# Banded attention with global keys and a two-matmul MoE layer: the second matmul of granules 4 to 11 as seven block products per granule pair

## The chip, the cores and the metric

The kernel runs on one core of one Trainium2 chip. The time is device microseconds of one execution; before the change it is 216.85 us, the median of three runs (216.78 to 217.0). The engines are called as the profile calls them: PE (TensorE, matrix multiply, with its weight loads as PEld), DVE (VectorE), ACT (ScalarE), POOL (GpSimd) and SP (SyncE, here only a queue that issues DMAs).

## The reference

Attention over 4 batches, 8 heads, 768 positions and 64 dimensions per head. A query sees the 96 positions up to and including its own, and the first 8 positions (global keys) always. A bias of minus a head's slope times the distance is added. The result, laid out as 3072 tokens of 512 features, goes through a feed-forward layer with a squared relu:

```python
scores = scale * q @ k.T + bias          # kept where global or local
a = softmax(scores); x = a @ v           # -> [3072, 512]
h = x @ w_in                             # [3072, 2048]
r = maximum(h, 0)
g = s * (r * r) + b
out = g @ w_out                          # [3072, 512]
```

## The kernel before

**Granules and steps.** The 3072 tokens are cut into 12 granules of 256 tokens (two blocks of 128), three to a batch. For attention a granule has four units, one per pair of heads. Two units are one step, so granule j fills steps 2j and 2j+1, and there are 24 steps (0 to 23). The program's order is written out by hand (`tc.manual_schedule()`), engine by engine; each engine works through its own list strictly in order and waits on semaphores.

**Attention.** `stage_S` multiplies queries and keys into the PSUM tile `ps_s` (L395), ACT takes the exponential into `pt` (L404), DVE multiplies with `tmpl`, the exponential of bias and mask (L411). `stage_A` multiplies `pt` with the values into `ps_av` (L446); the values carry a column of ones, so the row sum comes along. `normalize` takes its reciprocal (L419) and scales into `xn` (L420). From granule 4 on, `xn` is transposed to `xT` by DMAs on SP (L550), and the raw keys and queries too (`qk_by_dma`, L311).

A query block needs its own key block, and the block before it. The first rows of that earlier block lie outside the window, so their place is taken by the 8 global keys. For the granules that are not the first of their batch, `make_koff` and `make_voff` build these shifted blocks on DVE: a copy of the earlier block (L330 keys, L349 values) and then a copy of the 8 global columns or rows over it (L333, L353).

**The two MoE matmuls.** `p1_mm` is the first: eight groups per granule, each of two 128-column chunks of `w_in` times four 128-row parts of x, 256 tokens wide, so 8 matmuls of 128x256 (L566) into one PSUM bank. ACT applies the relu into `gT` (L576), DVE squares it in place (L579). `p2_mm` is the second: per block of 128 tokens, 16 matmuls of 128x512 (L611), with a block of `gT` as the stationary operand and `w_out` moving. `p2_out` scales by s and adds the vector `bvec` (b times the column sums of `w_out`) on DVE (L622) and stores 256 KB through SP (L631). `bvec` comes from `wsum_add` (L589, 15 additions spread through the opening) and `emit_bvec`. Granules 0 and 1 finish their second matmul before s and b are there, so `p2_hold` keeps the raw product and `p2_late` (L644) finishes it.

**PSUM.** Of eight banks, four hold scores (two units), one holds `ps_av`, and three (`ps_h`, tag `psh`) are shared by the groups of the first matmul, the second matmul and the transposes. A bank is handed on in the order in which the banks before were released in the program.

**A step.** `step(s, c0, c1, c2)` writes: the scores of step s+1 with their exponentials and masks; the pieces c0; `stage_A` of the step's first unit; the held-back outputs (`flush`); c1; `stage_A` of the second unit; c2 and, at a granule's end, `finish_granule` (transposes of `xn`, then the loads of the granule four ahead on POOL's queue). In the steady state a step has one `p2` block in c0 and two groups of the first matmul each in c1 and c2. After step 23 the rest of the MoE work follows without attention: the last block of granule 9, half of granule 10's first matmul, and granules 10 and 11. The very last block is cut by columns in 384 and 128 (`moe_p2_cols`, L668, L676).

Of the kernel before, what the change touches and what calls it, by code (L numbers as in the profile page):

```python
# [17 lines left out]
def kernel(  # L18
# [41 lines left out]
    gpool = ctx.enter_context(tc.tile_pool(name="gpool", bufs=4))  # L60
# [59 lines left out]
    for i in range(GB):  # L120
        f = work.tile([P, H, D], F32, name="first_v", tag="first_v", bufs=2)
        nc.sync.dma_start(f[:], rows_of(v, 0, i))
        first_v.append(f)
# [20 lines left out]
    idle = const.tile([P, 4 * P], BF16, name="idle")  # L144
# [20 lines left out]
    rel = const.tile([P, 2 * P], F32, name="rel")  # L165
# [25 lines left out]
    )  # L191
    ident_bf = const.tile([P, P], BF16, name="ident_bf")
    make_identity(nc, ident_bf[:])
    nat_tile(0)
    load_granule(1)
    for i in range(4):
        load_w_in(i, 4)
# [9 lines left out]
    base_bf = const.tile([P, 3, P], BF16, name="base_bf")  # L207
    nc.vector.tensor_copy(base_bf[:, 0, :], rel[:, 0:P])
    nc.vector.tensor_copy(base_bf[:, 1:3, :], rel[:].rearrange("p (a c) -> p a c", a=2))
    nc.vector.tensor_scalar_max(base_bf[0:NG, 0, :], base_bf[0:NG, 0, :], -float(NL))  # L210
    nc.vector.memset(base_bf[0:NG, 2, :], -float(NL))
    slopes = [float(2.0 ** (-8.0 * (h + 1) / H)) for h in range(H)]
    diag = const.tile([P, H, P], BF16, name="diag")
# [7 lines left out]
    tmpl = const.tile([P, H, 5, P], BF16, name="tmpl")  # L221

    def template(hs):
        for h in hs:
            nc.scalar.activation(tmpl[:, h, 0:3, :], base_bf[:, 0:3, :], ACT.Exp, scale=slopes[h])

    def template_rest(hs):
        nc.vector.tensor_copy(tmpl[:, hs, 3, :], tmpl[:, hs, 2, :])
        nc.scalar.copy(tmpl[:, hs, 4, :], tmpl[:, hs, 1, :])
# [14 lines left out]
    koff = {}  # L244
    voff = {}
# [9 lines left out]
    def qk_tile(b):  # L255
        if b not in qk:
            qk[b] = qkp.tile([P, 2, NB, HP, P], BF16, name="qk", tag="qk")
        return qk[b]

    def qk_by_pe(j, h2s=range(HP // 2), evac=(nc.vector.tensor_copy, nc.vector.tensor_copy)):  # L260
        b, g = divmod(j, NGR)
        t = qk_tile(b)
        for h2 in h2s:
            for n in range(2):
                ps = ps_h.tile([P, GB, 2, P], BF16, name="ps_t", tag="psh")
                for i in range(GB):
                    for c in range(2):
                        hp = 2 * h2 + c
                        nc.tensor.transpose(  # L269
                            ps[:, i, c, :],  # L270
                            nat[j][:, n, i, 2 * hp : 2 * hp + 2, :],
                            ident_bf[:],
                        )
                dst = t[:, n, g * GB : (g + 1) * GB, 2 * h2 : 2 * h2 + 2, :]
                if j == 0:

                    evac[n](
                        dst.rearrange("p b c (m s) -> p c b m s", s=GB),
                        ps[:].rearrange("p s c (b m) -> p c b m s", b=GB),
                    )  # L280
                else:
                    evac[n](dst, ps[:])

    def qk_block(j, i, evac):
        b, g = divmod(j, NGR)
        t = qk_tile(b)
        for n in range(2):
# [5 lines left out]
            evac[n](t[:, n, g * GB + i, :, :], ps[:])  # L293

    def qk_wide(j, n, evac):
        b, g = divmod(j, NGR)
        t = qk_tile(b)
# [6 lines left out]
        evac(t[:, n, g * GB : (g + 1) * GB, :, :], ps[:])  # L304

    def qk_by_dma(j):
        b, g = divmod(j, NGR)
        t = qk_tile(b)
        for i in range(GB):
            for n in range(2):  # L310
                nc.sync.dma_start_transpose(  # L311
                    t[:, n, g * GB + i, :, :],
# [4 lines left out]
    def make_koff(j, blocks=range(GB), h2=None, copy=nc.vector.tensor_copy, splice=True):  # L317
        b, g = divmod(j, NGR)
        if g == 0:
            return  # L320
        r0 = g * GB - 1
        t = qk_tile(b)
        if j not in koff:
            koff[j] = work.tile([P, GB, HP, P], BF16, name="koff", tag="koff", bufs=2)
        ko = koff[j]
        hs = slice(0, HP) if h2 is None else slice(2 * h2, 2 * h2 + 2)
        nh = HP if h2 is None else 2
        i0, n = blocks[0], len(blocks)
        if copy:
            copy(ko[:, i0 : i0 + n, hs, :], t[:, 0, r0 + i0 : r0 + i0 + n, hs, :])  # L330
        if not splice:
            return
        nc.vector.tensor_copy(  # L333
            ko[:, i0 : i0 + n, hs, 0:NG],
            t[:, 0, 0, hs, 0:NG].unsqueeze(1).to_broadcast((P, n, nh, NG)),
        )

    def make_voff(j, blocks=range(GB), copy=nc.vector.tensor_copy, splice=True):
        b, g = divmod(j, NGR)
        if g == 0:  # L340
            return
        r0 = g * GB - 1
        vn = vbuf[b % 2]
        if j not in voff:
            voff[j] = work.tile([P, GB, H, VW], BF16, name="voff", tag="voff", bufs=2)
        vo = voff[j]
        i0, n = blocks[0], len(blocks)
        if copy:
            copy(vo[:, i0 : i0 + n, :, :], vn[:, r0 + i0 : r0 + i0 + n, :, :])  # L349
        if not splice:  # L350
            return
        for i in blocks:
            nc.vector.tensor_copy(vo[0:NG, i, :, :], vn[0:NG, 0, :, :])  # L353

    def stage_S(u):
        j, hp, b, g = unit(u)
        t = qk_tile(b)
# [8 lines left out]
        c0 = 0 if first else 1  # L368
# [11 lines left out]
        plan = [(i, t[:, 0, r0 + i, hp, :], t[:, 1, r0 + i, hp, :]) for i in range(GB)]  # L380
        if first:
            plan.append((2, t[:, 0, 0, hp, :], t[:, 1, 1, hp, :]))
        else:
# [3 lines left out]
                (1, koff[j][:, 0, hp, :], t[:, 1, r0, hp, :]),  # L387
                (2, koff[j][:, 1, hp, :], t[:, 1, r0 + 1, hp, :]),
# [36 lines left out]
    def stage_A(u, pool=None):  # L425
# [10 lines left out]
        dcol, ocol = ((0, 1), (None, 2)) if first else ((0, 3), (1, 2))  # L436
        for i in range(GB):
            for hi in range(2):
                h = 2 * hp + hi
                terms = [(dcol[i], vn[:, g * GB + i, h, 0 : D + 1])]  # L440
                if not first:
                    terms.append((ocol[i], voff[j][:, i, h, 0 : D + 1]))
                elif i == 1:
                    terms.append((2, vn[:, 0, h, 0 : D + 1]))
# [14 lines left out]
    def block_S(j, i, pr):  # L459
        b, g = divmod(j, NGR)  # L460
        t = qk_tile(b)
# [4 lines left out]
        for n in range(2):  # L466
            for hi in range(2):
# [3 lines left out]
                    rhs=base_bf[:, 1:3, :],  # L471
# [4 lines left out]
        def scores():  # L476
            for n in range(2):
                hp = 2 * pr + n
                for o, kt in enumerate((t[:, 0, sb, hp, :], koff[j][:, i, hp, :])):
                    for hi in range(2):  # L480
# [5 lines left out]
                            rhs=t[rows, 1, sb, hp, :],  # L486
# [7 lines left out]
    def block_A(j, i):  # L494
# [3 lines left out]
        for pr in range(HP // 2):  # L498
# [5 lines left out]
            for n in range(2):  # L504
                for hi in range(2):
                    h = 4 * pr + 2 * n + hi
                    for o, vv in enumerate((vbuf[b % 2][:, g * GB + i, h], voff[j][:, i, h])):
# [43 lines left out]

    def moe_p1(j, fp):
# [4 lines left out]
    def p1_mm(j, fp):  # L557

        if j not in gT:
            gT[j] = gpool.tile([P, FC, GT], BF16, name="gT", tag="gT")  # L560
        g = gT[j]
# [23 lines left out]
    wsum = const.tile([P, DM], F32, name="wsum")  # L585

    def wsum_add(i):
        a_ = w_out_bf[:, 0, :] if i == 1 else wsum[:]
        nc.vector.tensor_tensor(wsum[:], a_, w_out_bf[:, i, :], ALU.add)  # L589

    hi = const.tile([P, DM], BF16, name="wsum_hi")
    lo = const.tile([P, DM], BF16, name="wsum_lo")

    def split_wsum():
        nc.scalar.copy(hi[:], wsum[:])
        nc.vector.tensor_tensor(lo[:], wsum[:], hi[:], ALU.subtract)

    def emit_bvec():
        ps = ps_h.tile([P, DM], F32, name="ps_b", tag="psh")
        nc.tensor.matmul(ps[:], lhsT=ones_bf[:], rhs=hi[:], start=True, stop=False)  # L600
        nc.tensor.matmul(ps[:], lhsT=ones_bf[:], rhs=lo[:], start=False, stop=True)
# [4 lines left out]
    def p2_mm(j, tb, lo=0, hi=FC):  # L606
# [3 lines left out]
        for fc in range(lo, hi):  # L610
            nc.tensor.matmul(  # L611
                po[:],
                lhsT=gT[j][:, fc, tb * P : (tb + 1) * P],
# [5 lines left out]
    def p2_out(j, tb):  # L619
        b, g = divmod(j, NGR)  # L620
        o_sb = work.tile([P, DM], F32, name="o_sb", tag="o_sb")
# [14 lines left out]
    def p2_hold(j, tb):  # L636
        o_sb = work.tile([P, DM], F32, name="o_early", tag="o_early", bufs=6)
# [22 lines left out]
    def moe_p2_cols(j, tb, parts):  # L660
# [3 lines left out]
        for c0, w in parts:  # L664
            cs = slice(c0, c0 + w)
            po = ps_h.tile([P, w], F32, name="ps_2c", tag="psh")
            for fc in range(FC):
                nc.tensor.matmul(  # L668
                    po[:],
                    lhsT=gT[j][:, fc, tb * P : (tb + 1) * P],  # L670
# [15 lines left out]


# [26 lines left out]
    def step(s, c0, c1, c2, pool=None):  # L714
# [5 lines left out]
        run(scores(s + 1))  # L720
        if not last and j not in voff:
            make_voff(j)
# [3 lines left out]
        if not last and QK_PE <= j + 1 < NJ:  # L726
            make_koff(j + 1)
        run(c1)
        stage_A(2 * s + 1, pool)
        n = 2 if j < X_PE else 1  # L730
# [3 lines left out]
        run(c2[n:])  # L734

# [32 lines left out]
    make_koff(1, [0])  # L768
    cast_v(1, cp)
    open_scores((2, 3))  # L770
    qk_block(1, 0, (cp, cp))
# [9 lines left out]
    make_koff(1, [1])  # L781
# [5 lines left out]
    make_voff(1, [0])  # L787
    make_voff(1, [1])
# [39 lines left out]
    make_koff(2)  # L828
    make_voff(2)
# [10 lines left out]
    run(s5)  # L840
    qk_by_dma(4)
# [21 lines left out]
    stage_A(14)  # L863
    stage_A(15, ps_h)
    q0()
    make_koff(4)
# [3 lines left out]
    make_voff(4)  # L870
# [11 lines left out]
    step(11, [lambda: p2_mm(3, 1, 0, FC // 2)], p1[4][0:2], late[2:4] + p1[4][2:4])  # L882
    step(12, [lambda: rest(3, 1)], p1[4][4:6], p1[4][6:8])
    step(13, p2[4][0:1], p1[5][0:2], p1[5][2:4])
    for j in range(7, NJ):
        step(2 * j, p2[j - 3][1:2], p1[j - 2][4:6], p1[j - 2][6:8])
        step(2 * j + 1, p2[j - 2][0:1], p1[j - 1][0:2], p1[j - 1][2:4])
    run(p2[NJ - 3][1:2])
    flush()
    run(p1[NJ - 2][4:8])  # L890
    for c in p2[NJ - 2]:
        c()
        flush()
    run(p1[NJ - 1])
    moe_p2(NJ - 1, 0)
    flush()
    moe_p2_cols(NJ - 1, 1, [(0, 3 * P), (3 * P, DM - 3 * P)])


# [33 lines left out]
```

The softmax here doesn't subtract the row's maximum and nothing guards it: scores larger than these inputs give would overflow.

## Time and profile before

| what | value |
|---|---|
| time, median of 3 runs | 216.85 us |
| the profiled execution, first to last instruction (its span) | 215.4 us |
| PE busy | 209.8 us, 97% |
| DVE busy | 140.5 us, 65% |
| ACT busy | 113.6 us, 53% |
| first MoE matmul, L566 | 768 matmuls of 128x256 |
| second MoE matmul, L611 and L668 | 368 of 128x512, 32 of 128x384 or 128x128 |
| relu, L576 | 96 of 598 ns |
| square, L579 | 96 of 424 ns |
| outputs, L622 | 19 of 744 ns |

The trace gives no separate figure for the profiled execution beyond its span; the 1.45 us between span and median time lie around it. In the profile's group lines come the source line, the engine, the operation, the tiles out<-in, the shapes, the count; after the first bar the busy time in us and the mean of one in ns; after the second the idle time of that engine in front of the group and what ended most of it. Matmul durations overlap each other, so a group's busy time of PE is more than the time it takes. In the chain, shares are of the span, traced back from the last instruction.

### The profile page before, as it was taken

To read this page: it belongs to the slowest core of one execution; us is meant where nothing else is said; L and a number is where in the kernel's file an instruction comes from. 1 tells how busy PE (TensorE), PEld (TensorE's weight loads), DVE (VectorE), ACT (ScalarE), POOL (GpSimd) and SP (SyncE) were. 2 spreads that over 40 slices of the span, in tenths; PEclk is the share of its full clock that TensorE was granted. 3 is DMA by queue.
4 is the path that set the end of the run, shared out by engine and by line. 5 is a ranking of instruction groups with operands and counts; after the bars stand their busy time and mean duration, and the time that the engine had idled before them with its cause. 6 is when DMAs were issued, how large, how long until landed. Compare 5 with 4: busy or idle time off the path is not lost.

```text
span 215.4 us, 4939 instructions
## 1 busy us (share of the span) xinstructions
PE 209.8 (97%) x2013; PEld 143.8 (67%) x2013; DVE 140.5 (65%) x344; ACT 113.6 (53%) x175; POOL 67.0 (31%) x89
## 2 busy tenths in 40 slices
PE   6999999999999999999999999999999999999993
PEld 2578885557866575776676676676676676665852
DVE  3497579995989668985675675666676663432421
ACT  4675668585975564554644643544644642240610
POOL 8873335897646104506318045000000000000000
PEclk9999999999999999999999999999999999999999
DMA  5999999999999997999999949952310310311102
GB/s 166 197 177 206 207 206 173 152 152 127 117 150 138 157 183 110 156 255 171 208 133 171 171 79 159 132 102 72 97 50 5 97 52 24 73 52 49 49 3 97
DMA packets 107079, 27.33 MB, mean 127 GB/s; under 512 B 97712, under 2 KB 104112, under 8 KB 107056
## 3 DMA queue, kind: packets, MB, share of 16 engines
q0 software_dynamic: 72864, 12.85, 82.2%
q1 hardware_dynamic: 33136, 13.64, 34.5%
q10 hardware_dynamic: 1056, 0.52, 0.9%
q8 instruction: 16, 0.26, 0.5%
q14 instruction: 7, 0.06, 0.1%
HBM read 27.26 MB, written 6.29 MB: 156 GB/s over the span
## 4 chain that ended last, share of the span: by engine, by line
PE 91%; DVE 5%; DMA 2%; issue 0%
PE ps L566 38%; PE ps L611 35%; PE ps_s L395 5%; PE ps_av L446 5%; DMA first<-in_k_dram 2%; PE ps_2c L668 2%; DVE pt L411 1%; PE ps_t L269 1%; PE ps_s L372 1%; PE ps_w L155 1%; PE ps_s L468 1%; PE ps_x L542 1%; PE ps_t L301 1%; DVE o_early L644 1%; DVE wsum L589 1%; DVE xn L420 1%
## 5 line engine op out<-in xcount | busy, mean ns | idle before, releaser
L576 ACT ACTIVATE gT<-ps 128x512 bf16<-128x512 f32 x96 | 57.0, 598 | 76.4 <-PE ps L566 76.4
L566 PE MATMUL ps<-xT,w_in_bf 128*128 128x256 bf16 x768 | 90.2, 273 | 0.0
L611 PE MATMUL ps<-w_out_bf,gT 128*128 128x512 bf16 x368 | 83.9, 380 | 0.0
L566 PEld LDWEIGHTS <-w_in_bf 128*128 128x128 bf16 x768 | 72.7, 98 | 8.9
L611 PEld LDWEIGHTS <-gT 128*128 128x128 bf16 x368 | 34.4, 98 | 39.2
L579 DVE TENSOR_TENSOR gT<-gT 128x512 bf16<-128x512 bf16 x96 | 40.4, 424 | 24.2 <-ACT gT L576 22.2
L404 ACT ACTIVATE pt<-ps_s 128x1024 bf16<-128x1024 f32 (+1 forms) x44 | 39.2, 948 | 6.4 <-PE ps_s L395 6.4
L411 DVE TENSOR_TENSOR pt<-pt,tmpl 128x1024 bf16<-128x1024 bf16 (+1 forms) x40 | 25.6, 650 | 9.3 <-ACT pt L404 8.6
L104 POOL DMA_DIRECT2D nat<-in_k_dram x22 | 19.7, 895 | 8.1 <-DMA w_in_bf<-in_moe_w_in_dram 3.0
L104 POOL DMA_DIRECT2D nat<-in_q_dram x22 | 19.6, 891 | 8.3 <-DMA w_out_bf<-in_moe_w_out_dram 3.4
L105 POOL DMA_DIRECT2D vb<-in_v_dram x22 | 19.8, 900 | 5.7 <-DMA w_out_bf<-in_moe_w_out_dram 2.1
L420 DVE TENSOR_TENSOR xn<-ps_av,rc 128x256 bf16<-128x256 f32 x48 | 20.4, 425 | 1.7
L622 DVE SCALAR_TENSOR_TENSOR o_sb<-ps,s_bc,bvec 128x512 f32<-128x512 f32 x19 | 14.1, 744 | 9.9 <-PE ps L611 9.9
L446 PEld LDWEIGHTS <-pt 128*128 128x128 bf16 x320 | 14.6, 97 | 5.9 <-DVE xn L420 0.8
L419 DVE RECIPROCAL rc<-ps_av 128x4 f32<-128x4 f32 x48 | 8.5, 178 | 14.8 <-PE ps_av L446 13.5
L446 PE MATMUL ps_av<-vb,pt 128*128 128x65 bf16 x208 | 15.4, 193 | 0.4 <-DVE xn L420 0.2
L110 POOL COPY gate<-xT 1x1 bf16<-1x1 bf16 x6 | 1.2, 202 | 40.6 <-DMA xT<-xn 37.9
L446 PE MATMUL ps_av<-voff,pt 128*128 128x65 bf16 x112 | 10.5, 193 | 0.0
L395 PE MATMUL ps_s<-qk 64*128 64x128 bf16 x208 | 10.0, 224 | 0.0
L589 DVE TENSOR_TENSOR wsum<-wsum,w_out_bf 128x512 f32<-128x512 f32 x14 | 9.6, 686 | 0.2
L395 PEld LDWEIGHTS <-qk 64*128 64x128 bf16 x208 | 6.2, 96 | 5.3 <-issue 3.2
L155 PE MATMUL ps_w<-idle 128*128 128x256 bf16 (+1 forms) x19 | 5.2, 434 | 1.2 <-DVE idle L145 1.2
(77 smaller groups left out, 107.6 us busy)
## 6 DMA issues: line engine op xcount, KB each, us to landing
out_dram<-o_sb SPq DMA_DIRECT2D x19, 256.0 KB, 3.5
nat<-in_k_dram POOLq DMA_DIRECT2D x22, 128.0 KB, 7.5
nat<-in_q_dram POOLq DMA_DIRECT2D x22, 128.0 KB, 7.4
vb<-in_v_dram POOLq DMA_DIRECT2D x22, 128.0 KB, 7.5
w_in_bf<-in_moe_w_in_dram POOLq DMA_DIRECT2D x4, 512.0 KB, 11.6
w_out_bf<-in_moe_w_out_dram POOLq DMA_DIRECT2D x4, 512.0 KB, 17.9
out_dram<-o_early SPq DMA_DIRECT2D x4, 256.0 KB, 6.6
first<-in_q_dram ACTq DMA_DIRECT2D x2, 256.0 KB, 4.9
```

The lines of the kernel that those rows point to most:

```text
L104: nc.gpsimd.dma_start(t[:, n, i, :, :], rows_of(srcs[n], b, sb))
L105: nc.gpsimd.dma_start(vbuf[b % 2][:, sb, :, 0:D], rows_of(v, b, sb))
L395: nc.tensor.matmul(ps[:, hi, oc * P : (oc + 1) * P], lhsT=kt[rows], rhs=qt[rows], start=not bias, stop=not bias or part * GB + n == len(pl ...
L404: nc.scalar.activation(pt[:, :, 0:ncol], ps[:, :, 0:ncol], ACT.Exp, scale=QSCALE)
L411: nc.vector.tensor_tensor(pv, pv, m.rearrange("p h a c -> p h (a c)"), ALU.mult)
L420: nc.vector.tensor_tensor(dst, av[:, :, :, 0:D], rc[:].to_broadcast((P, 2, 2, D)), ALU.mult)
L446: nc.tensor.matmul(av[:, i, hi, 0 : D + 1], lhsT=pt[:, hi, c * P : (c + 1) * P], rhs=vv, start=(n == 0), stop=(n == len(terms) - 1),)
L566: nc.tensor.matmul(ps[:, i, :], lhsT=w_in_bf[:, kc, fc * P : (fc + 1) * P], rhs=xT[j][:, kc, :], start=(kc == 0), stop=(kc == KC - 1),)
L576: nc.scalar.activation(gs, ps[:], ACT.Relu)
L579: nc.vector.tensor_tensor(gs, gs, gs, ALU.mult)
L611: nc.tensor.matmul(po[:], lhsT=gT[j][:, fc, tb * P : (tb + 1) * P], rhs=w_out_bf[:, fc, :], start=(fc == 0), stop=(fc == FC - 1),)
L622: nc.vector.scalar_tensor_tensor(out=o_sb[:], in0=po_cur.pop((j, tb))[:], scalar=s_bc[:], in1=bvec[:], op0=ALU.mult, op1=ALU.add,)
```

## The change

**Seven products.** For the pairs of granules (4,5), (6,7), (8,9) and (10,11) the second matmul is taken as a 2x2 block product: rows are the even and the odd granule (256 tokens each), the inner dimension is cut in two halves of 1024 and the columns in two halves of 256. Winograd's form of Strassen's scheme forms four sums of the activations (`g_sum`), four of the weights (`weight_sums`, once; one of them in place of a quarter of `w_out_bf`) and seven products of 256 x 1024 x 256 (`product`: 16 matmuls of 128x256 each). `evac` takes each product out of PSUM, six of them on DVE with the scale s and an addend, the seventh on ACT; `join` adds intermediate results in f32; four stores of 256 KB per pair go out.

**Order.** From step 13 on the order is new (the loop over `pr`): per pair four steps with products 1; 7 and 2; 5 and 6; 3 and 4, between two-group units of the first matmul (`unit_p1`). A unit's square is one operation over 1024 columns: on ACT for even granules, on DVE for odd ones. The last pair follows after step 23, with product 3 cut by blocks at the end. `step` gets a list `pre`, whose work stands on DVE between the exponentials and the masks, and further flushes.

**Keys and values.** The tile `qk` is split in `kx` and `qx`. Behind each key block stand the 8 global keys (`attach`, one copy per batch), so that a slice that begins 8 columns late is the shifted block. Templates get a fourth base and a sixth block for that order; the fourth base is made on POOL. The shifted values come by two DMAs on SP (`load_voff`: 120 rows, and 8 rows of global values).

**Memory.** To make room, tiles that are used only early share memory with later ones (`idle`, `rel`, `open_bf`, `wsum` with the activation sums; `first_v` with the outputs; `o_early` with `first`), and `gT` now holds a pair, in two buffers.

```diff
-    gpool = ctx.enter_context(tc.tile_pool(name="gpool", bufs=4))
+    gpool = ctx.enter_context(tc.tile_pool(name="gpool", bufs=2))
...
+    nc.gpsimd.affine_select(
+        out=base_bf[:, 3, :],
+        in_=rel[:, P - NG : 2 * P - NG],
...
-    tmpl = const.tile([P, H, 5, P], BF16, name="tmpl")
+    tmpl = const.tile([P, H, 6, P], BF16, name="tmpl")
...
+    def k_off(b, r, hp):
+        return qk[b][0][:, r, hp, NG : P + NG]
+
+    def attach(b, lo, hi):
+        kx = qk[b][0]
+        nc.vector.tensor_copy(
+            kx[:, lo:hi, :, P : P + NG],
+            kx[:, 0, :, 0:NG].unsqueeze(1).to_broadcast((P, hi - lo, HP, NG)),
+        )
...
+    def load_voff(j, blocks=range(GB)):
...
+        nc.sync.dma_start(vo[0 : P - NG, i0 : i0 + n], vn[NG:P, r0 + i0 : r0 + i0 + n])
+        nc.sync.dma_start(
+            vo[P - NG : P, i0 : i0 + n], vn[0:NG, 0].unsqueeze(1).to_broadcast((NG, n, H, VW))
+        )
...
-    def make_koff(j, blocks=range(GB), h2=None, copy=nc.vector.tensor_copy, splice=True):
...
-    def make_voff(j, blocks=range(GB), copy=nc.vector.tensor_copy, splice=True):
...
+    weight_sums = [
+        lambda: nc.vector.tensor_tensor(t1, w12, w11, ALU.subtract),
+        lambda: nc.vector.tensor_tensor(t2, w22, t1, ALU.subtract),
+        lambda: nc.vector.tensor_tensor(t3, w22, w12, ALU.subtract),
+        lambda: nc.vector.tensor_tensor(t4, w21, t2, ALU.subtract),
+    ]
...
+    def g_sum(pr, n, c=None):
...
+            dst, x, y, op = {
+                1: (s1, quarter(o, 0, c), quarter(o, 1, c), ALU.add),
+                2: (s2, s1, quarter(e, 0, c), ALU.subtract),
+                3: (s3, quarter(e, 0, c), quarter(o, 0, c), ALU.subtract),
+                4: (s4, quarter(e, 1, c), s2, ALU.subtract),
+            }[n]
+            nc.vector.tensor_tensor(dst, x, y, op)
...
+    def unit_p1(j, q):
+        for fp in (2 * q, 2 * q + 1):
+            relu, _ = p1_mm(j, fp)
+            relu()
+        gs = g_of(j)[:, 4 * q : 4 * q + 4, :]
+        if j % 2:
+            nc.vector.tensor_tensor(gs, gs, gs, ALU.mult)
+        else:
+            nc.scalar.activation(gs, gs, ACT.Square)
...
+    def product(pr, n, tbs=range(GB), ps=None):
...
+        for tb in tbs:
+            for fc in range(NH):
+                nc.tensor.matmul(
+                    ps[:, tb, :],
+                    lhsT=stat[:, fc, tb * P : (tb + 1) * P],
+                    rhs=mov[:, fc, :],
...
+    def evac(pr, n):
...
+        if n == 1:
+            scaled(res[pr][0][:], ps3, both_blocks(bvec[:, 0:CH]))
+        elif n == 2:
+            store(pr, 0, 0, ps, r0)
+        elif n == 5:
+            scaled(res[pr][1][:], ps3, both_blocks(bdiff[:]))
+        elif n == 6:
+            scaled(r0, ps, r0)
+        elif n == 7:
+            nc.scalar.activation(r7, ps, ACT.Copy, scale=s_bc[:])
+        elif n == 3:
+            store(pr, 0, 1, ps, r1)
+        elif n == 4:
+            store(pr, 1, 0, ps, r0)
...
+    def join(pr, n):
+            if n == 1:
+                add_f32(r1, r1, r0)
+            elif n == 0:
+                add_f32(r0, r0, r7)
+            else:
+                o = work.tile([P, GB, CH], F32, name="o_q", tag="o_sb", bufs=3)
+                add_f32(o[:].rearrange("p a c -> p (a c)"), r7, r1)
+                put(pr, 1, 1, o[:])
...
-    def step(s, c0, c1, c2, pool=None):
+    def step(s, c0, c1, c2, pool=None, pre=()):
...
+        run(exps)
+        run(pre)
+        run(masks)
...
-    for j in range(7, NJ):
-        step(2 * j, p2[j - 3][1:2], p1[j - 2][4:6], p1[j - 2][6:8])
-        step(2 * j + 1, p2[j - 2][0:1], p1[j - 1][0:2], p1[j - 1][2:4])
...
+        [u1(4, 0)],
+        late[2:4] + [u1(4, 1), weight_sums[0]],
+    )
+    step(12, [lambda: rest(3, 1)], [u1(4, 2), weight_sums[1]], [u1(4, 3), bias_diff, weight_sums[2]])
+    for pr in range(2, NJ // 2):
...
+        step(k0, [pe(pr, 1), u1(o, 0)], [u1(o, 1), g_sum(pr, 3, 0)], [])
+        step(
+            k0 + 1,
+            [u1(o, 2), pe(pr, 7)],
+            [u1(o, 3)],
+            [g_sum(pr, 1), pe(pr, 2)],
+            pre=[g_sum(pr, 3, 1)],
+        )
+        step(
+            k0 + 2,
+            [g_sum(pr, 2), u1(e + 2, 0), pe(pr, 5)],
+            [g_sum(pr, 4, 0), pe(pr, 6)],
+            [g_sum(pr, 4, 1), u1(e + 2, 1), join(pr, 1)] + [weight_sums[3]] * (pr == 2),
+        )
...
+        step(
+            k0 + 3,
+            [pe(pr, 3), flush, pe(pr, 4)],
+            [join(pr, 2), u1(e + 2, 2)],
+            [u1(e + 2, 3)],
+            pre=[join(pr, 0)],
+        )
...
+    run([u1(e, 2), u1(e, 3), pe(pr, 1), flush])
+    run([u1(o, 0), g_sum(pr, 3, 0), u1(o, 1), g_sum(pr, 3, 1)])
+    run([u1(o, 2), g_sum(pr, 1, 0), g_sum(pr, 2, 0), pe(pr, 7), flush])
+    run([u1(o, 3), g_sum(pr, 1, 1), g_sum(pr, 2, 1), pe(pr, 2), flush])
+    run([pe(pr, 5), flush, g_sum(pr, 4), pe(pr, 6), flush, join(pr, 1), join(pr, 2), join(pr, 0)])
+    run([pe(pr, 4), flush])
+    for tb in range(GB):
+        ps = ps_sc.tile([P, GB, 4 * P], F32, name="ps_last", tag="sc")
+        product(pr, 3, [tb], ps[:, :, 0:CH])
...
```

## The prediction

> **What bounds the kernel now.** I read the page's busy times and clock first, then the chain, then the costliest groups, then the timeline of one steady step, and last the waits and the end of the run.
>
> ```profile
> PE 209.8 (97%) x2013; PEld 143.8 (67%) x2013; DVE 140.5 (65%) x344; ACT 113.6 (53%) x175; POOL 67.0 (31%) x89
> PEclk9999999999999999999999999999999999999999
> PE 91%; DVE 5%; DMA 2%; issue 0%
> L576 ACT ACTIVATE gT<-ps 128x512 bf16<-128x512 f32 x96 | 57.0, 598 | 76.4 <-PE ps L566 76.4
> L566 PE MATMUL ps<-xT,w_in_bf 128*128 128x256 bf16 x768 | 90.2, 273 | 0.0
> L611 PE MATMUL ps<-w_out_bf,gT 128*128 128x512 bf16 x368 | 83.9, 380 | 0.0
> ```
>
> TensorE is the bound: 97% busy, full clock, 91% of the chain, no idle time in front of either MoE matmul. So matmul time taken away shortens the run, as long as nothing makes TensorE wait. What one matmul really costs is its pitch, not its mean of 273 or 380 ns (they overlap). The timeline of one step shows it:
>
> ```profile
> 168.68 0.40 PE L395 MATMUL ps_s<-qk 64*128 64x128 bf16 x8
> 169.24 3.63 PE L611 MATMUL ps<-w_out_bf,gT 128*128 128x512 bf16 x16
> 169.28 1.94 ACT L404 ACTIVATE pt<-ps_s 128x1024 bf16<-128x1024 f32 x2
> 170.33 0.69 DVE L411 TENSOR_TENSOR pt<-pt,tmpl 128x1024 bf16<-128x1024 bf16 x1 [0.49 <-ACT pt L404]
> 171.25 0.69 DVE L411 TENSOR_TENSOR pt<-pt,tmpl 128x1024 bf16<-128x1024 bf16 x1 [0.22 <-ACT pt L404]
> 172.95 1.91 PE L566 MATMUL ps<-xT,w_in_bf 128*128 128x256 bf16 x16
> 174.94 1.91 PE L566 MATMUL ps<-xT,w_in_bf 128*128 128x256 bf16 x16
> 176.69 0.59 PE L611 MATMUL ps<-w_out_bf,gT 128*128 128x512 bf16 x2
> ```
>
> From 169.24 to 172.95 lie 16 matmuls of 512 columns and 8 attention-value ones (0.25): 3.46/16 = 216 ns. From 174.94 to 176.69 lie 16 of 256: 1.75/16 = 109 ns, each with new weights. A step is 0.1 gap, scores 0.55, 3.46, 0.25, 1.75, 0.25, 1.75 = 8.1 us, and nothing in it waits.
>
> **The change part by part.**
>
> *The products.* A granule pair had 64 matmuls of 512: 64 x 216 = 13.82 us. Now it has 7 x 16 = 112 of 256: 112 x 109 = 12.21. Four pairs: **-6.45 us**.
>
> The Trainium skill ("TensorE: Matmul & The Clock Gate", Back-to-back issue gap) speaks against it: sustained pairs of weight load and matmul take some 131 ns at 512 columns and 81 at 128. By estimate, on the line between them, that is 98 at 256; a pair goes from 64 x 131 = 8.4 to 112 x 98 = 11.0 us, and four pairs add 10.4 us. The rows here say 216 and 109, almost exactly two to one, and decide.
>
> *What VectorE and ScalarE get.* Rows for it:
>
> ```profile
> L579 DVE TENSOR_TENSOR gT<-gT 128x512 bf16<-128x512 bf16 x96 | 40.4, 424 | 24.2 <-ACT gT L576 22.2
> L411 DVE TENSOR_TENSOR pt<-pt,tmpl 128x1024 bf16<-128x1024 bf16 x28 | 19.1, 690 | 8.0 <-ACT pt L404 8.0
> L622 DVE SCALAR_TENSOR_TENSOR o_sb<-ps,s_bc,bvec 128x512 f32<-128x512 f32 x19 | 14.1, 744 | 9.9 <-PE ps L611 9.9
> L589 DVE TENSOR_TENSOR wsum<-wsum,w_out_bf 128x512 f32<-128x512 f32 x14 | 9.6, 686 | 0.2
> ```
>
> A bf16 two-source operation grows by 0.266 per 512 elements, so 2048 cost 1.22. The f32 row sets the other end: 0.686 grows to 2.28. All operands are bf16, so I take 1.22. VectorE per pair before: 16 squares 6.8, 8 masks 5.5, 8 normalisations (0.18 + 0.42) 4.8, 4 outputs 3.0, shifted copies 2.4: 22.5 in 32.4 us. After: 4 squares of 1024 2.8, masks and normalisations 10.3, four operand sums 5.2 (two in halves), six evacuations 4.5, three f32 joins 2.1, the attached keys 0.2: 25.1 in an ideal 30.75 us, 82%. ScalarE gains four squares of 1024 (nearest row: a bf16 copy of that size, 1.05; low end the exponentials' 1.03) and one evacuation 0.6, 17.8 to 22.6. Neither is the bound by sum. What counts is order, since every product needs a sum or a free PSUM bank on time.
>
> I lay one pair out with these durations (0 = end of the last first-matmul group; a relu starts 0.21 after its group; an independent VectorE operation starts 0.08 before its forerunner ends).
>
> - First step: scores to 0.65, product 1 to 2.4, two groups to 4.14, attention-value to 4.39, two groups to 6.13. ScalarE must square the even granule's last quarter first (to 1.98), so the exponentials end at 3.82 and the masks at 4.54. The odd granule's first square waits for its relu (4.95) and ends at 5.69, reciprocal and normalise end at 6.25. The second attention-value matmuls (one PSUM bank) are due at 6.13 and start at 6.31: **0.2**.
> - Second step: product 7 is due at 8.95; the second half of its operand sum (square 6.99-7.68, half sums, a normalisation between) ends at 9.46. First half: four matmuls. **0.25**.
> - Third step: the sum behind product 5 ends at 16.2, evacuation of product 2 at 16.85, masks at 18.3, the sum for product 6 at 19.43; product 6 is due at 19.31. **0.25**.
> - Fourth step: products 3 and 4, evacuations at 28.45 and 29.67, the banks are due at 28.6 and 29.72: none, but with 0.1 to spare.
>
> So 0.7 per pair for granules 4/5 and 6/7, 0.45 for 8/9 (its third step has no masks), 0.35 in step 12, where a square precedes the exponentials and the normalisation follows the masks, 0.4 after step 23 (products 7 and 5 wait for half sums): **+2.6**. The weight sums (4 x 1.22) stand where granule 4's squares stood (8 x 0.424, now on ScalarE); the fourth ends at 25.5, product 4 needs it at 25.7: 0, or 1.1 if it is 2.28.
>
> *The end.*
>
> ```profile
> 208.41 3.66 PE L668 MATMUL ps_2c<-w_out_bf,gT 128*128 128x384 bf16 x32
> 211.86 0.96 SPq L684 DMA_DIRECT2D out_dram<-o_part  x2
> 212.10 0.35 DVE L676 SCALAR_TENSOR_TENSOR o_part<-ps_2c,s_bc,bvec 128x128 f32<-128x128 f32 x1 [0.28 <-PE ps_2c L668]
> ```
>
> Today VectorE ends 0.37 after TensorE. Now one evacuation, three joins, one evacuation and two halves (4.5) follow product 6, beside 3.5 of products 4 and 3: it ends 1.25 after. The last store is 128 KB behind 256 KB (2.3 to landing) where 64 KB (1.6) stood. **+1.2**, bounds 0.5 and 2.0.
>
> *Shifted keys and values.* koff and voff cost VectorE 14.6 us in all, none of it in front of TensorE but near 46 us (mask behind copies) : **-0.2**. The attached keys are 0.25 per batch. Values now come by DMA on SP. From granule 4 on they are issued about two steps (16 us) ahead, past transposes of 5.6 and outputs of 3.5 to landing: nothing. For granule 1 the first goes out at 11.5 and is needed at 17.0, the second at 13 and 19.4. Landing is bounded by 1.6 (64 KB, idle engines) and 8.6 (the tiny scalars behind transposes); first_v, twice the bytes at the same hour, took 6.8, so half of the bytes near 5: on time, **0**, at worst +1.4. While SP waits there nothing else is due on it before 49 us. POOL's extra select (0.4) delays the weight loads; the DMA engines' backlog there hides it, else +0.4. Wider templates (8 x 0.1 on ScalarE, at 34 to 40 us) hide behind the second matmul of granule 0. Tiles that share memory are free again long before reuse: 0.
>
> Sum: -6.45 + 2.6 + 1.2 - 0.2 = -2.85. The profiled execution spans 215.4, the median is 216.85; the 1.45 around the span I keep: 215.4 - 2.85 = 212.55, **214.0 us**.
>
> **The rivals.**
>
> *The gain arrives whole.* My waits of 0.2 to 0.25 are as large as my reading errors. With 0.6 of them left and 0.8 at the end: 216.85 - 6.45 + 0.6 + 0.8 - 0.2 = 211.6. For it: today's waits on TensorE are almost nil. Against: five tight meetings per pair.
>
> *VectorE's sums set the pace (slower).* Place: products 6 and 7, which wait for sums of 2048 and halves. At 1.22 a pair loses 0.7. Each 0.1 more per 2048 costs 0.2 at product 6 and 0.1 at product 7. From about 1.5 a pair loses its 1.6. At 1.75 (midway to the f32 end): waits of 2.3 a pair, 7.6 in all, 216.85 - 6.45 + 7.6 + 1.2 - 0.2 = 219.0. Against: the squares and masks, same operation and type.
>
> *The opening stalls.* If granule 1's values take first_v's 6.8 us, TensorE waits 1.4 at 17 us: 215.4.
>
> *No net change.* Twice my waits and the upper end cost: 216.85 - 6.45 + 5.2 + 1.5 - 0.2 = 216.9.
>
> **How the numbers follow.** Chances: forecast (213.0 to 215.0) 0.50, whole gain 0.19, opening 0.10, VectorE 0.17, no net change 0.04. A difference under about 0.2% (0.4 us) cannot be told from none. Faster takes the first three (0.78 with the edge taken off), same 0.03, slower 0.19. The range 211.2 to 217.6 leaves out the slower case's main part (0.15) and 0.05 below.
>
> **What would show it.** Right: 448 matmuls of 256 at 109 ns pitch; steps near 7.9 instead of 8.1; sums of 2048 near 1.22; TensorE waiting for gsum in front of products 6 and 7 for 0.2 to 0.3; VectorE ending 1.2 after TensorE. Wrong: sums above 1.5, TensorE idle at 17 to 20 us behind the value DMA, or banks waiting for the evacuations in the fourth step, where 0.1 is to spare.

## The result, and the profile after

The changed kernel takes 223.39 us (median of 4 runs, 221.23 to 224.7) against 216.85 us before. It is slower by 6.5 us, where 214.0 was forecast. The longest of the four counts as a slow run, so the ratio is taken from the other three (median 222.54): 1.026, 95% interval 1.021 to 1.032. The profiled execution is that longest one: its span is 222.9 us, 7.5 more than the 215.4 before, and its time is 2.2 us above the median of the other three, so the trace shows more loss than a usual run has.

Page of the changed kernel: busy times, the rows of the 40 slices for TensorE's granted clock (9 is full speed) and the DMA engines, the chain, one of the costliest groups, and the shifted values' DMAs (count, size, median us from issue to landing).

```profile
PE 205.8 (92%) x2189; PEld 161.6 (72%) x2189; DVE 149.8 (67%) x309; ACT 132.4 (59%) x195; POOL 67.3 (30%) x90
PEclk9999999999999589999999999999999999999999
DMA  6999999999999993499999997996364021240014
PE 55%; DMA 32%; DVE 4%; SPq 3%; POOL 2%; issue 2%; ACT 1%; POOLq 0%; DVEq 0%; ACTq 0%
L445 PE MATMUL ps_av<-vo,pt 128*128 128x65 bf16 x112 | 10.7, 197 | 6.5 <-DMA vo<-vb 6.5
vo<-vb SPq DMA_DIRECT2D x7, 247.5 KB, 7.5
```

TensorE's work has become less (205.8 us for 209.8), but it is busy for 92% of the span where it was 97%. A third of the chain now is DMA, where it was 2%. The clock, full in every slice before, has two slices below that, and the DMA row shows where they lie: at the end of a first third in which the DMA engines are full. Much of this could be read before the change. Here are three lines of that profile: the DMA row of its page, SP's timeline from 40 to 70 us, and the time to landing in the view of its key and query transposes (L311):

```profile
DMA  5999999999999997999999949952310310311102
54.99 15.63 SPq L311 DMA_TRANSPOSE qk<-nat  x7
DMA to landing us min/median/max: 2.4/5.6/9.5
```

The first 15 slices were full there too, SP went through seven transposes from 55 to 70 us, and a transpose took up to 9.5 us to land.

What TensorE waited for (waits view; total us, times, longest):

```profile
PEld L445 <- DMA vo<-vb: 7.1, 3, 5.7
PE ps_av L445 <- DMA vo<-vb: 6.5, 3, 5.4
PE ps_av L508 <- DMA vo<-vb: 1.4, 1, 1.4
PEld L768 <- DVE gsum L732: 1.2, 5, 0.3
PE ps_s L394 <- DMA qx<-nat: 0.9, 1, 0.9
```

The products wait for VectorE's operand sums five times, 0.3 us at most, as forecast. The long waits stand in front of attention-value matmuls and are for `vo`, the shifted values. (PEld is the weight load in front of the same matmul, so its line shows the same wait.)

To see when the time went, I took the start of the scores' first matmul in each step from the timelines. A step's scores are those of half a granule, so equal work lies ahead of them in both kernels, except the products from step 13 on.

| us | before | after | after minus before |
|---|---|---|---|
| scores of step 8 (granule 4) | 61.53 | 63.00 | 1.47 |
| scores of step 9 | 64.35 | 66.84 | 2.49 |
| scores of step 10 (granule 5) | 70.93 | 80.92 | 9.99 |
| scores of step 12 (granule 6) | 83.62 | 93.61 | 9.99 |
| scores of step 16 (granule 8) | 112.50 | 122.31 | 9.81 |
| scores of step 20 (granule 10) | 144.52 | 153.23 | 8.71 |
| scores of step 23 | 168.68 | 176.08 | 7.40 |
| TensorE's last matmul ends | 212.07 | 218.33 | 6.26 |
| VectorE's last result | 212.46 | 219.92 | 7.47 |

Ten microseconds are lost before step 10, before any product has run. From there TensorE wins back 3.73, and the end gives 1.21 of that away. The largest loss, 7.5 us between steps 9 and 10, is one place. Timeline of the changed kernel (start, us, engine, line, instruction, in brackets the idle time before it):

```profile
51.06 0.91 POOL L104 DMA_DIRECT2D nat<-in_k_dram  x1
...
58.19 1.32 SPq L350 DMA_TRANSPOSE kx<-nat  x1
59.61 1.28 SPq L350 DMA_TRANSPOSE qx<-nat  x1
61.18 1.50 SPq L350 DMA_TRANSPOSE kx<-nat  x1
62.77 1.90 SPq L350 DMA_TRANSPOSE qx<-nat  x1
...
64.76 0.90 SPq L298 DMA_DIRECT2D vo<-vb  x1
...
69.13 0.19 PE L445 MATMUL ps_av<-vb,pt 128*128 128x65 bf16 x1
...
74.73 0.24 PE L445 MATMUL ps_av<-vo,pt 128*128 128x65 bf16 x1 [5.40 <-DMA vo<-vb]
...
75.10 3.60 PE L569 MATMUL ps<-xT,w_in_bf 128*128 128x256 bf16 x16
...
78.96 2.03 PE L569 MATMUL ps<-xT,w_in_bf 128*128 128x256 bf16 x16
```

Granule 4's values are issued at 64.76, behind the four transposes of granule 5, which occupy SP from 58.19 on: each takes 1.3 to 1.9 us to issue, and only the third also waits, 0.2 us, for POOL's load of 51.06, which lands at 61.16. The values are needed at 69.13, 4.4 us after their issue. They take some 9.5 us to land. TensorE stands for 5.40 us, and the sixteen matmuls that follow take 3.60 us instead of the 1.91 that they take elsewhere: the clock has been halved. TensorE's rows over time (length, busy us and matmuls, granted clock, the DMA packets' times as a share of 16 engines' time, GB/s; the share passes 1 because the times of packets add up even where they overlap) say the same:

```profile
60.00:70.00 10.00, 8.47 (x92) 1.00 1.86 129
70.00:80.00 10.00, 5.27 (x40) 0.66 1.96 161
80.00:90.00 10.00, 10.00 (x108) 1.00 0.76 118
```

So the place costs 5.4 us of waiting and 2.1 us at half clock. The other losses are the values of granules 1 and 2 (TensorE waits 1.38 us from 16.72 and 0.35 us up to 47.70) and the transposes of granule 4 (0.85 us at 63.2).

The end, by the timeline:

```profile
213.79 1.22 DVE L732 TENSOR_TENSOR gsum<-gT,gsum 128x2048 bf16<-128x2048 bf16 x1
214.67 1.91 PE L768 MATMUL ps<-wsub,gT 128*128 128x256 bf16 x16
...
216.42 1.91 PE L768 MATMUL ps_last<-w_out_bf,gsum 128*128 128x256 bf16 x16
...
219.44 0.48 DVE L777 SCALAR_TENSOR_TENSOR o_last<-ps_last,s_bc,part 128x256 f32<-128x256 f32 x1 [0.48 <-DMA out_dram<-o_q]
```

From 214.67 to 216.42 lie sixteen matmuls of 256 columns: 1.75/16 = 109 ns. The 2048-element sum takes 1.22 us. VectorE ends 1.60 us after TensorE, where it was 0.39.

### The profile page after: what moved, and what is told of

Same layout as the page of the kernel before. It is cut to its first block, busy times and chain, and to the rows that moved or that the text cites. A ratio compares the mean times of both kernels' runs of the same rounds, so it can differ in the third digit from the quotient of the medians.

```text
span 222.9 us, 5309 instructions
## 1 busy us (share of the span) xinstructions
PE 205.8 (92%) x2189; PEld 161.6 (72%) x2189; DVE 149.8 (67%) x309; ACT 132.4 (59%) x195; POOL 67.3 (30%) x90
## 4 chain that ended last, share of the span: by engine, by line
PE 55%; DMA 32%; DVE 4%; SPq 3%; POOL 2%; issue 2%; ACT 1%; POOLq 0%; DVEq 0%; ACTq 0%
PE ps L569 26%; PE ps L768 19%; DMA vo<-vb 10%; DMA nat<-in_k_dram 8%; DMA vb<-in_v_dram 7%; DMA w_in_bf<-in_moe_w_in_dram 6%; PE ps_av L445 4%; PE ps L617 3%; PE ps_s L394 3%; SPq L350 2%; SPq L298 1%; DMA out_dram<-o_q 1%; POOL nat L104 1%; DVE xn L419 1%; ACT pt L403 1%
## 5 line engine op out<-in xcount | busy, mean ns | idle before, releaser
L569 PE MATMUL ps<-xT,w_in_bf 128*128 128x256 bf16 x768 | 92.2, 276 | 0.0
L617 PE MATMUL ps<-w_out_bf,gT 128*128 128x512 bf16 x128 | 29.7, 380 | 0.0
L768 PEld LDWEIGHTS <-gsum 128*128 128x128 bf16 x256 | 24.2, 98 | 4.4 <-DVE gsum L732 1.2
L617 PEld LDWEIGHTS <-gT 128*128 128x128 bf16 x128 | 11.8, 98 | 13.0
L768 PEld LDWEIGHTS <-gT 128*128 128x128 bf16 x192 | 18.3, 98 | 2.4
L582 DVE TENSOR_TENSOR gT<-gT 128x512 bf16<-128x512 bf16 x32 | 13.4, 423 | 8.9 <-ACT gT L579 8.6
L743 DVE TENSOR_TENSOR gT<-gT 128x1024 bf16<-128x1024 bf16 x16 | 11.1, 691 | 11.0 <-ACT gT L579 10.8
L745 ACT ACTIVATE gT<-gT 128x1024 bf16<-128x1024 bf16 x16 | 16.9, 1057 | 0.5
L445 PE MATMUL ps_av<-vo,pt 128*128 128x65 bf16 x112 | 10.7, 197 | 6.5 <-DMA vo<-vb 6.5
L768 PE MATMUL ps<-w_out_bf,gT 128*128 128x256 bf16 x128 | 15.3, 273 | 0.0
L768 PE MATMUL ps<-wsub,gsum 128*128 128x256 bf16 x128 | 15.3, 273 | 0.0
## 6 DMA issues: line engine op xcount, KB each, us to landing
vo<-vb SPq DMA_DIRECT2D x7, 247.5 KB, 7.5
```

The costliest lines, as they stand in the source:

```text
L445: nc.tensor.matmul(av[:, i, hi, 0 : D + 1], lhsT=pt[:, hi, c * P : (c + 1) * P], rhs=vv, start=(n == 0), stop=(n == len(terms) - 1),)
L569: nc.tensor.matmul(ps[:, i, :], lhsT=w_in_bf[:, kc, fc * P : (fc + 1) * P], rhs=xT[j][:, kc, :], start=(kc == 0), stop=(kc == KC - 1),)
L582: nc.vector.tensor_tensor(gs, gs, gs, ALU.mult)
L617: nc.tensor.matmul(po[:], lhsT=g_of(j)[:, fc, tb * P : (tb + 1) * P], rhs=w_out_bf[:, fc, :], start=(fc == 0), stop=(fc == FC - 1),)
L745: nc.scalar.activation(gs, gs, ACT.Square)
L768: nc.tensor.matmul(ps[:, tb, :], lhsT=stat[:, fc, tb * P : (tb + 1) * P], rhs=mov[:, fc, :], start=(fc == 0), stop=(fc == NH - 1),)
```

## The experiments

Theory A: the products and their sums do about what was forecast, and the loss is the shifted values' DMAs in the first 80 us, through their place in SP's queue, through full DMA engines, and through the clock. Theory B: the products, sums and joins lose the time. Each kernel is the changed one with one edit, unless its heading says otherwise.

### The products alone

```diff
         run(masks)
+        if not last and j not in voff:
+            make_voff(j)
...
-        if not last and j % NGR == 0:
-            attach(j // NGR, 1, NB)
+        if not last and QK_PE <= j + 1 < NJ:
+            make_koff(j + 1)
```

All shifted keys and values, the templates and the key layout are those of before.

> The seven products and their operand sums as in the changed kernel, but shifted keys and values built on VectorE as before. Theory A (the values' DMAs cost all of the loss, the products gain about what was forecast): TensorE waits for no shifted values, granted clock 1.00, and the time is 216.85 - 3.85 + 1.2 = 214.2 us, up to 216 if VectorE's 2.7 us of shifted copies per granule get in front of the products' sums. Theory B (the products, their sums and joins cost the loss): near the changed kernel's 223 us.

Measured: 217.09 us, ratio to before 1.0005 (0.9996 to 1.0014). Until step 12 the steps start within 0.2 us of before, with the clock at 1.00. So the products don't lose the time, and B falls; but the gain isn't there either, and 217.09 lies above A's range. The waits view says why:

```profile
PE ps_av L447 <- DVE voff L354: 2.3, 4, 0.8
PEld L770 <- DVE gsum L734: 1.2, 5, 0.3
```

And VectorE's timeline of this kernel:

```profile
122.02 0.68 DVE L809 TENSOR_TENSOR part<-part,part 128x512 f32<-128x512 f32 x1
122.84 0.69 DVE L412 TENSOR_TENSOR pt<-pt,tmpl 128x1024 bf16<-128x1024 bf16 x1
123.76 0.69 DVE L412 TENSOR_TENSOR pt<-pt,tmpl 128x1024 bf16<-128x1024 bf16 x1 [0.22 <-ACT pt L405]
124.37 0.43 DVE L350 COPY voff<-vb 128x1056 bf16<-128x1056 bf16 x1
124.83 0.49 DVE L354 COPY voff<-vb 8x528 bf16<-8x528 bf16 x2
```

`make_voff` stands behind the masks and a join, and its 0.92 us come just when TensorE needs the values. Four such waits cost 2.3 us. TensorE ends 1.49 us before the kernel before (3.8 without these waits), and the longer end takes 1.2. In the kernel before, the waits view has no matmul that waits for these copies, and one weight load (0.4 us); beside the products they no longer hide.

### The shifted keys and values alone

```diff
-        [u1(4, 0)],
-        late[2:4] + [u1(4, 1), weight_sums[0]],
...
-    for pr in range(2, NJ // 2):
...
+    step(11, [lambda: p2_mm(3, 1, 0, FC // 2)], p1[4][0:2], late[2:4] + p1[4][2:4])
+    step(12, [lambda: rest(3, 1)], p1[4][4:6], p1[4][6:8])
+    step(13, p2[4][0:1], p1[5][0:2], p1[5][2:4])
...
```

From step 11 on the schedule is that of before.

> The new handling of shifted keys and values, but the second MoE matmul as before, 64 matmuls of 512 columns per granule pair. Theory A: all of the loss is here: the scores of granule 5 start 10 us later than in the kernel before (1.5 from the opening, 1.0 at the transposes of granule 4, 7.5 at its shifted values), nothing is won back, 224 to 227 us. Theory B: 216.5 to 217.5 us.

Measured: 226.7 us, ratio 1.045 (1.041 to 1.050). The scores of step 8 start 1.40 us later than before, those of step 9 2.58, those of step 10 10.66, and TensorE ends 10.9 later. A holds. The two halves don't add up (0.0 and +9.7, but +6.5 together). 2.3 of the 3.2 us between are explained: with the values off VectorE the products keep the 2.3 us that they lost alone. The rest is not separated from the scatter of the runs.

### Granule 4's values first

```diff
     stage_A(11)
+    load_voff(4)
...
     stage_A(14)
-    load_voff(4)
...
+        if not last and QK_PE < j + 1 < NJ:
+            load_voff(j + 1)
         if not last and j >= 4 and j + 2 < NJ:
             qk_by_dma(j + 2)
-        if not last and QK_PE < j + 1 < NJ:
-            load_voff(j + 1)
```

> The changed kernel with granule 4's shifted values issued right after granule 2's attention, ahead of granule 5's transposes on SP, and in each later step ahead of the transposes too. Theory A1 (the values were late because SP, in order, stood behind transposes that wait for granule 5's loads): they are issued near 58 us instead of 64.8, landed before 67, TensorE does not wait at 69 us and its clock stays at 1.00; 215 to 217 us, and the wait for granule 7's values at 117 us (0.7 us) is gone too. Theory A2 (they are late because the DMA rings are full at that time, whatever the order): they land after 70 us, and the time stays above 220 us.

Measured: 220.69 us, ratio 1.018 (1.016 to 1.020): the time is in A2's range, the trace is not. Its timeline:

```profile
58.21 0.91 SPq L298 DMA_DIRECT2D vo<-vb  x1
...
68.62 0.20 PE L445 MATMUL ps_av<-vo,pt 128*128 128x65 bf16 x1
...
74.63 0.57 PE L394 MATMUL ps_s<-qx,kx 64*128 64x128 bf16 x14 [1.74 <-DMA qx<-nat]
...
75.13 5.31 PE L617 MATMUL ps<-w_out_bf,gT 128*128 128x512 bf16 x15
```

As A1 said, the values go out at 58.2 and TensorE doesn't wait for them at 68.6. But the wait moves. Granule 5's transposes now stand behind the values, start 1.9 us later (60.09 for 58.19) and take 9.3 us to land (9.1 in the changed kernel); TensorE waits 1.74 us for them, and the clock drops again (15 matmuls of 512 columns take 5.31 us; 16 took 3.63 in the kernel before). Step 12 starts 5.3 us later than before instead of 10.0. So the order on SP was about half of the loss up to there.

### The loads of granules 6 and 7 held back

On top of the last edit:

```diff
-        if 6 <= j + LEAD < NJ:
-            hold_loads(xT[j][0:1, 0, GT - 1 : GT])
-            load_granule(j + LEAD)
+        held = {2: (), 3: (6,), 4: (7, 8)}.get(j, (j + LEAD,))
+        for n in held:
+            if 6 <= n < NJ:
+                hold_loads(xT[j][0:1, 0, GT - 1 : GT])
+                load_granule(n)
```

> The kernel with the values issued first, and the loads of granules 6 and 7 released one granule later each (behind granule 3's and granule 4's attention instead of granule 2's and 3's), so that they no longer run beside granule 4's values and granule 5's transposes. Theory A3 (between 55 and 75 us everything lands late because POOL's loads share the DMA engines): the transposes of granule 5, which took 9.1 and 9.3 us to land, take 4 to 6, TensorE does not wait 1.7 us at 73 us, the clock stays at 1.00, and the time falls from 220.7 to 217 to 218 us. Theory A4 (the values' own DMAs and the transposes on SP's queue hold each other up, whatever POOL loads): the wait at 73 us stays, 220 to 221 us.

Measured: 225.32 us, ratio 1.037 (1.030 to 1.044). Where it was aimed it did what A3 said: granule 5's transposes land in 5.9 to 7.0 us, there is no wait at 73 us, and the clock is full until 107 us. But the time is more than 7 us above what was expected, because the same loads collide later. Granules 7 and 8 are now loaded together at 86 to 97 us, and there (timeline):

```profile
102.34 0.57 PE L394 MATMUL ps_s<-qx,kx 64*128 64x128 bf16 x14 [2.30 <-DMA qx<-nat]
109.27 2.08 PE L569 MATMUL ps<-xT,w_in_bf 128*128 128x256 bf16 x9 [4.50 <-DMA xT<-xn]
```

So POOL's loads in the same window are a good part of what makes a transfer land late (9.3 us with them, 5.9 to 7.0 without), and they can't simply be moved.

### The wait filled

```diff
-    idle = gpool.tile([P, 4 * P], BF16, name="idle", tag="gsum1", bufs=1)
+    idle = const.tile([P, 4 * P], BF16, name="idle")
...
         run(c0)
+        if s == 8:
+            warm(24, 4 * P)
         stage_A(2 * s)
```

`warm` issues matmuls on the tile `idle` whose result nobody reads; that tile needs memory of its own now, since it shared that of an activation sum.

> The changed kernel with 24 idle matmuls of 512 columns (5.2 us) where TensorE waits for granule 4's shifted values at 69 us. Theory C (the wait costs twice: 5.4 us of idle time, and then 2.1 us at half clock, because TensorE had stood still): the granted clock stays at 1.00 through 60 to 80 us, the matmuls after the wait keep their pitch of 109 ns, and the time falls by about 2 us against the changed kernel. Rival D (the clock fell for a reason of its own, not for the idle time): the clock falls as before, and the time is the same or 0.3 us more.

Measured: 222.87 us, ratio to before 1.027 (1.025 to 1.030). TensorE's rows over the same time:

```profile
60.00:70.00 10.00, 8.68 (x93) 1.00 1.92 127
70.00:80.00 10.00, 9.89 (x88) 1.00 1.88 165
80.00:90.00 10.00, 9.95 (x89) 1.00 0.95 144
```

and the matmuls after the wait:

```profile
74.99 1.91 PE L569 MATMUL ps<-xT,w_in_bf 128*128 128x256 bf16 x16
```

C holds: the clock stays, and the scores of step 10 start at 78.82 instead of 80.92, 2.1 us earlier, and it stays so (2.4 at step 23). The idle time itself halves the clock. The times don't show a gain, though 2 us were expected: the medians differ by 0.5, and the ratios to before are 1.027 here and 1.026 for the changed kernel. The two traces compared are the longest run of the changed kernel and the shortest of this one, so the 2.1 us can't be put down to the edit alone. One reading is that the changed kernel's own wait is shorter in its other runs (they spread over 3.5 us), while the 24 matmuls always take 5.2 us; here the values landed at 73.66, 1.1 us before the next work starts. That reading was not tried.

### Early values on VectorE, late ones by DMA

```diff
+    EARLY = (1, 2, 4, 5)
...
     def k_off(b, r, hp):
+        j, i = b * NGR + (r + 1) // GB, (r + 1) % GB
+        if j in EARLY:
+            return koff[j][:, i, hp, :]
         return qk[b][0][:, r, hp, NG : P + NG]
...
-        if g == 0:
+        if g == 0 or j in EARLY:
             return
```

`make_koff` and `make_voff` are called for these granules where they were before; the templates hold both key orders (7 columns for 6); the select for the shifted one is issued behind the weight loads; in a step the values go ahead of the transposes.

> The products as in the changed kernel; shifted keys and values of granules 1, 2, 4 and 5 on VectorE as before, those of granules 7, 8, 10 and 11 by DMA and behind the keys (values issued ahead of the transposes). Theory A (the DMAs are late only in the first 80 us, where the loads fill the DMA engines; later they cost nothing, and they spare the products the 2.3 us that TensorE waited for VectorE's voff with the products alone): until 95 us the steps start where they did before, then TensorE gains 3.8 us, less 1.2 at the end: 214.0 to 214.8 us. Theory B (the values' DMAs also cost later): TensorE waits for vo or the transposes after 100 us, 216 us or more.

Measured: 214.56 us, ratio 0.989 (0.986 to 0.993): A's number, and faster than the kernel before, by 1.1%. Steps 8 to 12 start within 0.1 us of before. In the profiled run, the longest of the four, TensorE ends 2.93 us earlier, with one wait left after 100 us, as B had it: 1.67 us up to 113.8 for the transposes of granule 6's normalised values.

### The end, and the last wait

The last two results in buffers that no store holds:

```diff
-        o = work.tile([P, CH], F32, name="o_last", tag="o_sb", bufs=3)
+        o = work.tile([P, CH], F32, name="o_last", tag="first", bufs=4)
```

> The same as the kernel with the early values on VectorE, and the last two results are written to buffers that no store in flight holds. VectorE's wait of 0.48 us in front of the last result goes: 0.4 to 0.5 us less than that kernel. If the last stores set the end, whatever VectorE does: no difference.

Measured: 214.38 us (one of the four runs took 218.65), ratio 0.988 (0.986 to 0.990). VectorE ends 1.03 us after TensorE instead of 1.60, but the medians lie 0.2 apart, inside both kernels' scatter, so the gain is seen in the trace and not in the times.

Then, with that, the later values behind the transposes again:

```diff
+        if not last and j == 6:
+            load_voff(j + 1)
         if not last and j >= 4 and j + 2 < NJ:
             qk_by_dma(j + 2)
+        if not last and 6 < j < NJ - 1:
+            load_voff(j + 1)
```

> The kernel with the early values on VectorE and the free last buffers; granule 7's values still issued ahead of the transposes of granule 8, but the values of granules 8, 10 and 11 behind the transposes again, as in the changed kernel. There TensorE waited 0.7 and 1.7 us at 113 us for granule 6's transposes, issued at 105.6 with granule 8's values right behind them at 108.7. If these values slowed the transposes, the wait goes and the time is 213.4 to 214.0 us. If the transposes are slow because of POOL's loads at 99 to 105 us, the wait stays at 0.7 to 1.7 us and the time near 214.4.

Measured: 214.49 us, ratio 0.988 (0.986 to 0.989). The wait stays, 0.93 us at 113.0. So granule 8's values weren't its cause. That POOL's loads are is only the branch left over; what makes this wait 0.3 to 1.7 us from run to run stays open.

And the last pair's addition for its fourth block on GpSimd:

```diff
-    def join(pr, n):
+    def join(pr, n, eng=nc.vector):
...
-    run([pe(pr, 5), flush, g_sum(pr, 4), pe(pr, 6), flush, join(pr, 1), join(pr, 2), join(pr, 0)])
+    run([pe(pr, 5), flush, g_sum(pr, 4), pe(pr, 6), flush, join(pr, 1), lambda: join(pr, 2, nc.gpsimd)(), join(pr, 0)])
```

> The same, with the last granule pair's addition for its fourth output block on GpSimd instead of VectorE. If VectorE's queue behind the last product sets the end, its last result comes 0.5 to 0.7 us sooner after TensorE's last matmul (1.03 us now) and the time falls by as much. If GpSimd's addition and its store end later than VectorE's, or the last store's way to DRAM counts alone, the time is the same or longer.

Measured: 214.8 us, ratio 0.990 (0.988 to 0.991). GpSimd takes 1.71 us where VectorE took 0.69. VectorE now ends 0.52 us after TensorE, but the span goes on for 4.4 us after that, where it was 3.5: the block's store starts at 207.46 and the last stores queue behind it. Relieving VectorE at the end bought nothing here.

## Why the prediction was wrong, point by point

- **Shifted values by DMA: 0.** This is the step that failed, in three ways. First, "issued about two steps (16 us) ahead" took the place in the program for the time of issue. SP took its list in order: granule 4's values stood behind four transposes that occupied it for 6.6 us, and had 4.4 us; moved ahead of them, they went out at 58.2 instead of 64.8. Second, the landing was bounded at 8.6 and then weighed against 16 us of slack; it was 9.5 at 65 us and 3.4 at 155 us. The 5.6 us for the transposes ahead of them was a median over the whole run, of which the longest was 9.5 even before the change. The row that tells the hours apart, the DMA engines' row of the page, shows nines for the first third, and I didn't read it. Third, a wait was priced at its length, but the clock took 2.1 us more. In the profiled run this place lost 7.5 us, and with granules 1 and 2 and the transposes below it is 10.0 by step 10.
- **Granule 1's values.** "On time, 0, at worst +1.4": they landed in 7.8 and 6.7 us, and TensorE waited 1.38. The estimate of 5 us scaled `first_v`'s 6.8 by its bytes, but `first_v` was issued at 1.8 and 2.4 us and the values at 10.2 and 12.1, and half of the bytes landed no sooner. The rival of the opening stall had the right place and price, but as something that could go wrong alone. Granules 2, 4 and 7 waited for their values too: 0.35, 5.40 and 0.72 us.
- **What else the new DMAs touch.** The transposes of granule 4 were issued 2.05 us later than before and cost 1.0. I had nothing on them. They waited for POOL's loads of that granule, which landed later than before; whether the extra select on POOL or the early values' DMAs held these loads up is not separated.
- **The products, -6.45.** The pitch is 109 ns. The rule from the Trainium skill that was weighed ("TensorE: Matmul & The Clock Gate", Back-to-back issue gap) would, by the estimate from it, have made the products cost 10.4 us; the rows decided, rightly.
- **The waits, +2.6.** TensorE wins 3.73 after step 10, 4.45 without the 0.72 us that it waits for granule 7's values. So 6.45 - 4.45 = 2.0 is left for the waits; 1.2 of it shows as waits for operand sums.
- **The end, +1.2.** VectorE's lag grew by 1.21, and the stores take as long as before (3.0 us).
- **VectorE's relief, -0.2.** The sign was right and the size far too small: 2.3 us depend on it, as the products alone show, which gained nothing without it.
- **VectorE's sums set the pace (the slower rival).** It fell: 1.22 us, as taken.

With the early values on VectorE, 214.4 to 214.6 was measured, close to the forecast of 214.0. Part of that is luck: in the trace the waits after step 10 are shorter than forecast (6.45 - 2.93 - 1.67 = 1.85 us for 2.6), and the wait for granule 6's transposes, which the forecast didn't have, makes up for it.

## What to carry to other kernels

A transfer that replaces an engine's copy must be priced by its hour: read from the DMA row whether the engines are full then, and from the queue's own timeline what the issuing instruction stands behind, not how far ahead it is written. Moving work from a busy engine to the DMA queues can be right in one half of a run and wrong in the other, so split the change by stage before judging it. And two edits that pay for each other have to be tried apart and together: here one alone gave nothing, the other lost 4.5%, and together, each in its place, they gave 1.1%.

## What the runs showed of the hardware

The trace's records of the granted clock change only on a grid of 3.413 us, and how much of one such window TensorE was idle goes with the clock of the next. Wherever the eleven traces have a record of the next window, a window idle for up to 49%, by the matmuls' records, was followed by the full clock, and one idle for 60% or more by the half. Between them, at 51 to 58%, both occurred. So a wait of 1.74 us that fell into one window halved the clock for 3.4 us (granule 5's transposes in the kernel with granule 4's values first, 52% idle), while one of 1.67 us in the kernel with the early values on VectorE did not (49%). The Trainium skill ("TensorE: Matmul & The Clock Gate", Part 1: The HAM clock gate) has the same free-running window of 3413 ns and says that the clock falls after an idle window; here a window that was half idle was enough.

The same 247.5 KB from SBUF to SBUF took 3.4 us to land at 155 us and 9.5 at 65 us, beside loads that had filled the DMA engines before the change too.
